# A long convolution between MLPs: the front half with taps on TensorE, the filter's transpose through DRAM, and an order written by hand

## The chip, the cores and the metric

The kernel runs on one core of a Trainium2 chip. The metric is the device time of one execution in microseconds (us), lower being better. Engine names: PE is TensorE, DVE VectorE, ACT ScalarE, POOL GpSimd, and SP SyncE, which here only issues DMAs.

## The reference

```python
def _A_ref(q, k, v, shift_k, ssm_k, ssm_D):
    ...
    for t in range(ks):
        k_shift = k_shift + k_pad[:, t:t + S, :] * shift_k[:, ks - 1 - t][None, None, :]
    kv = k_shift * v
    ...
    y_f = kv_f * kf_f[None, :, :, :]
    ...
    y = y + kv * ssm_D[None, None, :]
    return q * y

x = A_q
x = x + _A_ref(_layernorm(x, axis=-1), A_k, A_v, A_shift_k, A_ssm_k, A_ssm_D)
x = x + _B_ref(_layernorm(x, axis=-1), B_w1, B_b1, B_w2, B_b2)
x = x + _A_ref(_layernorm(x, axis=-1), A_k, A_v, A_shift_k, A_ssm_k, A_ssm_D)
x = x + _B_ref(_layernorm(x, axis=-1), B_w1, B_b1, B_w2, B_b2)
```

Sequence S = 2048, width D = 512, MLP width 1376, bf16. `kv` is a causal convolution of `k` over four taps, times `v`. It is then convolved over the whole sequence with a filter `ssm_k` of length 2048 per channel, by Fourier transforms; `_B_ref` is layernorm, a linear layer, GELU and a linear layer. The convolved `y` doesn't depend on x, so that it is worked out once for both layers.

## The kernel before

The 2048-point transform is done in two matmul stages. Stage 1 multiplies by `Ft` (the sum over 32 of the index's parts), a transpose of 32 x 32 blocks on VectorE brings the other part onto the partitions, and stage 2 multiplies by `Wt`, one 128 x 128 table for each of 32 values of k. This is done for the filter (`Kraw` -> `Ktok` -> `ZT` -> `ZK`) and for `kv` (`uv` -> `ZT` -> `ZX`). The x loop then takes the spectrum of `kv` two k at a time: `x_mul` (stage 2 into `px`, copied to `xb`, and two products with `ZK` and with `KSW`, which is `ZK` with its two halves of partitions swapped by DMA), and `x_inv` (the inverse table `Mt`, back into `ZX`). Four block transposes give `V2`, and matmuls with `Gt` give `YA` = y.

In order: all loads are issued from SP, ACT and POOL; `k_transpose` turns the filter on the PE; for each chunk `cc` of 128 channels `kv_chunk` makes the four taps on VectorE (products with a broadcast of `shift_k`, sums, product with `v`), then `stage1` is called for the filter and for `kv`. Then 16 `k_stage2`, 16 steps of the x loop with the first layernorm after the fourth, the inverse transposes, and 8 groups of the last stage. Behind that lies the MLP: `prep`, `ln_transpose`, `mm1`, `mm2` over 2 layers x 4 groups of 512 tokens. Within the program the scheduler of the language sets each engine's order; an engine works through its own queue in order, and PSUM tiles come from pools of two buffers, `pa` and `pb`.

## Time and profile before

| | us |
|---|---|
| median of 3 runs | 340.16 |
| lowest and highest | 338.97, 341.21 |
| the profiled execution | 341.24 |
| its span, first to last instruction | 339.2 |
| PE busy | 242.7 |
| VectorE busy | 225.4 |
| ScalarE busy | 164.4 |
| GpSimd busy | 19.8 |

The span is what the trace covers; the device time is 2.04 us longer. Busy times are sums over the whole span, in which stages with different limits follow one another, so a stage is read by itself. In the rows below a line number is that of the kernel before; `arena` is the one large SBUF tile in which most named buffers are placed, so that it stands for several of them. PEclk is the share of TensorE's full clock of 2.4 GHz that was granted, 0.50 being 1.2 GHz.

### The profile page before, as it was taken

Reading aid. Unit: us, or ns where it says so; the run is one execution under the profiler, and the core shown is the slowest. Engines: PE = TensorE matmul, PEld = TensorE weight load, DVE = VectorE, ACT = ScalarE, POOL = GpSimd, SP = SyncE. Lnnn points to the kernel's source line nnn. Section 1 sums busy time; section 2 is a strip of 40 time slices with the busy share of each in tenths; the row PEclk is TensorE's granted clock in tenths of the full one; section 3 lists DMA queues with packets and bytes.
Section 4 is the critical chain, followed back from the end, with each engine's and each line's share of the span. In section 5 each row is a group of like instructions: output and inputs, shape, how many; then the busy total and the mean of one; then the engine's idle time right before and its main releaser. Section 6 shows DMA issues by size and latency. Waiting matters only on the chain.

```text
span 339.2 us, 3467 instructions
## 1 busy us (share of the span) xinstructions
PE 242.7 (72%) x1292; PEld 122.0 (36%) x1312; DVE 225.4 (66%) x361; ACT 164.4 (48%) x206; POOL 19.8 (6%) x26
## 2 busy tenths in 40 slices
...
GB/s 228 372 389 4 2 0 2 0 0 247 144 255 225 122 166 166 0 0 0 2 0 0 3 0 0 2 0 1 3 0 0 2 0 46 17 41 21 18 62 46
DMA packets 7040, 21.94 MB, mean 65 GB/s; under 512 B 912, under 2 KB 4593, under 8 KB 5872
## 3 DMA queue, kind: packets, MB, share of 16 engines
...
q0 software_dynamic: 112, 0.00, 0.1%
...
## 4 chain that ended last, share of the span: by engine, by line
DVE 44%; PE 36%; DMA 8%; ACT 6%; POOL 3%; issue 2%; another core or an unknown queue 0%; DVEq 0%; POOLq 0%; ACTq 0%
PE po L328 17%; PE ph L316 14%; DVE arena L200 7%; DVE st L169 6%; DMA arena<-in_A_ssm_k_dram 6%; DVE arena L266 5%; DVE arena L177 4%; DVE kvm L159 3%; ACT arena L207 3%; DVE kvt L158 3%; DVE T L235 3%; POOL rs L173 3%; DVE arena L244 3%; DVE T L234 2%; DMA arena<-in_A_k_dram 2%
## 5 line engine op out<-in xcount | busy, mean ns | idle before, releaser
L328 PE MATMUL po<-arena 128*128 128x512 bf16 (+1 forms) x339 | 79.6, 379 | 1.9 <-DVE arena L331 1.2
L316 PE MATMUL ph<-arena 128*128 128x512 bf16 (+1 forms) x349 | 79.6, 387 | 0.8 <-ACT arena L308 0.7
L318 ACT ACTIVATE arena<-ph,B 128x512 bf16<-128x512 f32 (+1 forms) x88 | 60.3, 687 | 29.6 <-PE ph L316 27.6
L331 DVE TENSOR_TENSOR arena<-po,arena 128x512 bf16<-128x512 f32 x32 | 21.9, 683 | 50.1 <-PE po L328 50.1
L316 PEld LDWEIGHTS <-arena 128*128 128x128 bf16 (+1 forms) x352 | 35.8, 102 | 43.6 <-issue 4.2
L328 PEld LDWEIGHTS <-arena 128*128 128x128 bf16 (+1 forms) x352 | 33.8, 98 | 38.7 <-issue 1.3
L198 PE MATMUL pz<-arena,Ft 128*128 128x128 bf16 x256 | 26.1, 276 | 27.9 <-DVE arena L160 17.3
L169 DVE BATCH_NORM_STATS2 st<-arena 128x6 f32<-128x512 bf16 x64 | 42.4, 677 | 5.0 <-DMA arena<-in_A_q_dram 4.3
L199 ACT ACTIVATE ZT<-pz 128x1024 bf16<-128x1024 f32 x32 | 30.8, 1028 | 23.1 <-PE pz L198 22.7
L308 ACT ACTIVATE arena<-pt 128x512 bf16<-128x512 bf16 x32 | 17.3, 594 | 42.6 <-PE pt L307 39.5
L198 PEld LDWEIGHTS <-Ft 128*128 128x128 bf16 x256 | 22.9, 128 | 31.2 <-issue 26.9
L200 DVE STREAM_TRANSPOSE arena<-ZT 128x2048 f32<-128x2048 f32 x8 | 29.4, 3678 | 3.8 <-ACT ZT L199 3.8
L173 POOL TENSOR_TENSOR rs<-rs,mhalf 128x4 f32<-128x4 f32 x16 | 16.2, 1010 | 203.7 <-DVE rs L172 203.7
L187 PE MATMUL pk<-IDt,arena 128*128 128x128 bf16 x64 | 5.8, 265 | 27.8 <-DVE arena L143 26.7
L177 DVE TENSOR_SCALAR arena<-arena,rs,nm 128x512 bf16<-128x512 bf16 x64 | 22.1, 408 | 0.6
L273 PE MATMUL py<-arena,Gt 128*128 128x512 bf16 x31 | 9.4, 460 | 18.3 <-DVE arena L266 17.6
L242 PE MATMUL pv<-T,arena 128*128 128x512 bf16 x63 | 18.5, 392 | 3.4 <-DVE T L234 1.5
L274 ACT ACTIVATE arena<-py 128x1024 bf16<-128x1024 f32 x8 | 7.9, 1022 | 22.1 <-PE py L273 22.1
L232 ACT ACTIVATE xb<-px 128x1024 bf16<-128x1024 f32 x16 | 16.3, 1040 | 3.4 <-DVE T L235 3.3
L207 ACT ACTIVATE arena<-pk 128x1024 bf16<-128x1024 f32 x16 | 15.1, 1055 | 2.6 <-PE pk L206 2.6
L266 DVE STREAM_TRANSPOSE arena<-arena 128x2048 f32<-128x2048 f32 x4 | 16.2, 4151 | 0.1
L189 ACT ACTIVATE arena<-pk 128x2048 bf16<-128x2048 bf16 x4 | 7.2, 1882 | 18.4 <-PE pk L187 18.4
...
## 6 DMA issues: line engine op xcount, KB each, us to landing
arena<-arena SPq DMA_DIRECT2D x8, 512.0 KB, 7.7
...
arena<-in_A_ssm_k_dram ACTq DMA_DIRECT2D x4, 512.0 KB, 19.5
...
```

The costliest lines, as they stand in the source:

```text
L169: nc.vector.bn_stats(st[:, i, :], x_t[:, GT * g + i, :])
L173: nc.gpsimd.tensor_tensor(rs[:], rs[:], mhalf[:], ALU.pow)
L177: nc.vector.tensor_scalar(out=dst[:, i, :], in0=x_t[:, GT * g + i, :], scalar1=rs[:, i:i + 1], scalar2=nm[:, i:i + 1], op0=ALU.mult, op1=A ...
L198: nc.tensor.matmul(pz[:, i, :], Ft[:, q // 2, :], src[:, tau, c0:c0 + CW], start=True, stop=True)
L199: nc.scalar.activation(ZT[:, 8 * q:8 * q + 8, :], pz[:], AF.Copy)
L200: nc.vector.transpose(dst[:, :, c0:c0 + CW].bitcast(F32).rearrange("p k c -> p c k"), ZT[:].bitcast(F32).rearrange("p b c -> p c b"))
L207: nc.scalar.activation(ZK[:, 2 * j:2 * j + 2, :], pk[:], AF.Copy)
L266: nc.vector.transpose(V2[:, :, c0:c0 + CW].bitcast(F32).rearrange("p k c -> p c k"), ZX[:, :, c0:c0 + CW].bitcast(F32).rearrange("p b c -> ...
L316: nc.tensor.matmul(ph[0:m, :], W1t[:, ct, ft * P:ft * P + m], lt[:, ct, :], start=ct == 0, stop=ct == CT - 1)
L318: nc.scalar.activation(ht[0:m, ft, :], ph[0:m, :], AF.Gelu_apprx_tanh, bias=B1[0:m, ft:ft + 1])
L328: nc.tensor.matmul(po[:], ht[0:m, ft, i * P:(i + 1) * P], W2t[0:m, ft, :], start=ft == 0, stop=ft == FT - 1)
L331: nc.vector.tensor_tensor(xs, po[:], xs, ALU.add)
```

## The change

- Loads: the filter comes first on SP, then `k` in four parts, `v`, `Wt`, `Gt`; on ACT only the identity, `Ft` and the taps `sT` in 128 x 4 x 4. The broadcast `SKr`/`SK` and the shifted copy `kh` go.
- The taps: `kv_transpose` turns `k` on the PE into `kT`; GpSimd makes 16 diagonal matrices `DG`; `kv` accumulates four matmuls per tile in PSUM and VectorE multiplies the sum with `v`.
- The filter's stage 1 works on all 512 channels at a time (`k_filter_stage1`), writes its result to a buffer `Zd` in DRAM and reads it back transposed into `ZK`; the four block transposes of the filter on VectorE go.
- `kv`, stage 1 of `kv`, the block transposes and `k_stage2` are interleaved chunk by chunk. The x loop runs over two halves of 256 channels with four k per step and two steps in flight. Evictions are dealt to ScalarE (A) or VectorE (D) by the tables `E_...`.
- The statistics of the first layernorm stand behind the x loop, its scaling behind the inverse transposes.
- The order of PE, ACT and DVE in this half is that of the code (`manual_schedule`). The MLP and its order stay.

```diff
-    nc.sync.dma_start(SKr[:], apf(A_shift_k, 0, [[0, P], [1, D * KS]]))
-    nc.sync.dma_start(kh[:, KS - 1:, :], k_d.rearrange(TOK, p=P))
-    h = KS - 1
-    for p0, n in ((1, 112), (113, 15)):
-        nc.scalar.dma_start(kh[p0:p0 + n, 0:h, :], apf(k_d, (16 * p0 - h) * D, [[16 * D, n], [1, h * D]]))
-    nc.vector.memset(kh[0:1, 0:h, :], 0.0)
...
     nc.scalar.dma_start(IDt[:], ident_h.ap().bitcast(BF16))
+    nc.scalar.dma_start(Ft[:], F_h.ap().bitcast(BF16))
+    nc.scalar.dma_start(sT[:], A_shift_k.rearrange("(ct p) k -> p ct k", p=P))
     for ct in range(CT):
-        nc.scalar.dma_start(Kraw[:, ct, :], A_ssm_k[ct * P:(ct + 1) * P, :])
+        nc.sync.dma_start(Kraw[:, ct, :], A_ssm_k[ct * P:(ct + 1) * P, :])
+    for t4 in range(4):
+        nc.sync.dma_start(kn[:, 4 * t4:4 * t4 + 4, :], k_d.rearrange(TOK, p=P)[:, 4 * t4:4 * t4 + 4, :])
     nc.sync.dma_start(uv[:], v_d.rearrange(TOK, p=P))
...
-    nc.vector.tensor_copy(B1[:], b1T[:])
     nc.gpsimd.memset(mhalf[:], -0.5)
-    nc.vector.tensor_copy(SK[:], SKr[:].rearrange("p d k -> p k d"))
+    nc.vector.memset(kT[:, :, :, 0:2], 0.0)
     nc.vector.tensor_tensor(Kraw[:, :, 0], Kraw[:, :, 0], Dc[:], ALU.add)
...
-    def kv_chunk(cc):
-        c0 = cc * CW
-        m = rot.tile([P, NT, CW], BF16, name="kvm", tag="kvm")
...
-        nc.vector.tensor_tensor(m[:], kh[:, h:h + NT, c0:c0 + CW], sb(0), ALU.mult)
-        for t in range(1, KS):
-            m2 = rot.tile([P, NT, CW], BF16, name="kvt", tag="kvt")
-            nc.vector.tensor_tensor(m2[:], kh[:, h - t:h - t + NT, c0:c0 + CW], sb(t), ALU.mult)
-            nc.vector.tensor_tensor(m[:], m[:], m2[:], ALU.add)
-        nc.vector.tensor_tensor(uv[:, :, c0:c0 + CW], m[:], uv[:, :, c0:c0 + CW], ALU.mult)
...
+        def k_filter_transpose(t4):
+            pk = nxt(pa, [4, D], BF16)
...
+            evac(E_KT[t4], Ktok[:, t4 * 4:t4 * 4 + 4, :], pk[:])
+
+        def k_filter_stage1(q):
+            ZT = nxt(ZTb, [8, D])
+            for i2 in range(4):
+                pz = nxt(pb, [2, D])
+                for i in range(2):
+                    tau = 8 * (q % 2) + 2 * i2 + i
+                    nc.tensor.matmul(pz[:, i, :], Ft[:, q // 2, :], Ktok[:, tau, :], start=True, stop=True)
+                evac(E_S1K[q][i2], ZT[:, 2 * i2:2 * i2 + 2, :], pz[:])
+            for g in range(4):
+                nc.sync.dma_start(apf(Zd, (32 * g + 8 * q) * NA * D, [[D, 32], [NA * D, 8], [1, D]]),
+                                  ZT[32 * g:32 * g + 32])
...
+        def kv_transpose(t4):
+            pk = nxt(pa, [4, CT, P], BF16)
...
+            evac(E_kT[t4], kT[:, :, 4 * t4:4 * t4 + 4, 2:2 + P].rearrange("p ct i c -> p i ct c"), pk[:])
...
+        def kv(ct, o):
+            pu = nxt(pa, [8, P])
+            for i in range(8):
+                for t in range(KS):
+                    tau = 8 * o + i - t
+                    w = kT[:, ct, tau, 2:2 + P] if tau >= 0 else kT[:, ct, tau + NT, 1:1 + P]
+                    nc.tensor.matmul(pu[:, i, :], w, DG[:, ct, t, :], start=t == 0, stop=t == KS - 1)
+            us = uv[:, 8 * o:8 * o + 8, ct * P:(ct + 1) * P]
+            nc.vector.tensor_tensor(us, pu[:], us, ALU.mult)
...
+        def stage1(cc):
             c0 = cc * CW
...
+            ZT = nxt(ZTb, [NA, CW])
...
+                if q % 2 and cc < 3:
+                    kv(cc + 1, q // 2)
+                pz = nxt(pb, [8, CW])
...
+                    nc.tensor.matmul(pz[:, i, :], Ft[:, q // 2, :], uv[:, tau, c0:c0 + CW], start=True, stop=True)
+                evac(E_S1U[cc][q], ZT[:, 8 * q:8 * q + 8, :], pz[:])
+            return ZT
+
+        def z_transpose(cc, ZT):
+            c0 = cc * CW
+            nc.vector.transpose(ZX[:, :, c0:c0 + CW].bitcast(F32).rearrange("p k c -> p c k"),
                                 ZT[:].bitcast(F32).rearrange("p b c -> p c b"))
...
         def k_stage2(j):
-            pk = ps.tile([P, 2, D], F32, name="pk2", tag="pa")
+            pk = nxt(pb, [2, D])
...
-            nc.scalar.activation(ZK[:, 2 * j:2 * j + 2, :], pk[:], AF.Copy)
...
-        k_transpose()
-        for cc in range(NCH):
-            kv_chunk(cc)
-            stage1(Ktok, ZK, cc, "pa")
-            stage1(uv, ZX, cc, "pb")
-        Mt = place("Mt", [P, NA, 2, P], 96 * K)
-        nc.sync.dma_start(Mt[:], M_h.ap().bitcast(BF16))
...
-        for j in range(NA // 2):
-            k_stage2(j)
+            evac(E_K2[j % 4], ZK[:, 2 * j:2 * j + 2, :], pk[:])
...
-        x_t = place("x_t", [P, NT, D], 116 * K)
-        nc.sync.dma_start(x_t[:], q_d.rearrange(TOK, p=P))
...
+        def x_mul(j, c0, w):
+            n = 1024 // w
+            k0 = n * j
+            px = nxt(pa, [n, w])
+            for i in range(n):
+                nc.tensor.matmul(px[:, i, :], Wt[:, k0 + i, :], ZX[:, k0 + i, c0:c0 + w], start=True, stop=True)
+            xb = nxt(xbb, [n, w])
+            evac("A", xb[:], px[:])
+            T = nxt(Tb, [2, n, w])
+            nc.vector.tensor_tensor(T[:, 0], xb[:], ZK[:, k0:k0 + n, c0:c0 + w], ALU.mult)
+            nc.vector.tensor_tensor(T[:, 1], xb[:], KSW[:, k0:k0 + n, c0:c0 + w], ALU.mult)
             return T
...
-        pend = None
-        for j in range(NA // 2):
-            T = x_mul(j)
-            if pend is not None:
-                x_inv(j - 1, pend)
-            pend = T
-            if j == 3:
-                layernorm(lna0, 0)
...
+        def x_inv(j, c0, w, eng, T):
...
+                    nc.tensor.matmul(pv[:, i, :], Mt[:, k0 + i, r, :], T[:, r, i, :], start=r == 0, stop=r == 1)
+            evac(eng, ZX[:, k0:k0 + n, c0:c0 + w], pv[:])
...
+        E_KT, E_kT = "DDDD", "DDDD"
+        E_S1K = ["ADAA", "ADAA", "ADAA", "ADAA"]
+        E_S1U = ["AAAA", "AAAA", "AAAA", "AAAA"]
+        E_K2 = "AADA"
...
+        def step(j, c0, w, eng):
+            T = x_mul(j, c0, w)
+            pend.append((j, c0, w, eng, T))
+            if len(pend) > 2:
+                x_inv(*pend.pop(0))
...
+        with tc.manual_schedule(engines={ENG.PE, ENG.Activation, ENG.DVE}):
+            for t4 in range(4):
+                k_filter_transpose(t4)
+            nc.vector.tensor_copy(sF[:], sT[:])
+            for ct in range(CT):
+                for t in range(KS):
+                    nc.gpsimd.tensor_scalar(out=DG[:, ct, t, :], in0=IDt[:], scalar1=sF[:, ct, t:t + 1], scalar2=None,
+                                            op0=ALU.mult)
+            nc.vector.tensor_copy(B1[:], b1T[:])
+            for q in range(4):
+                k_filter_stage1(q)
+                kv_transpose(q)
+            for j4 in range(4):
+                nc.sync.dma_start(ZK[:, 8 * j4:8 * j4 + 8, :], apf(Zd, 8 * j4 * D, [[NA * D, P], [1, 8 * D]]))
+            kv(0, 0)
+            kv(0, 1)
+            zt = None
+            for cc in range(4):
+                if zt is not None:
+                    z_transpose(cc - 1, zt)
+                zt = stage1(cc)
+                if cc == 1:
+                    nc.scalar.dma_start(Mt[:], M_h.ap().bitcast(BF16))
+                if cc > 0:
+                    for j in range(4 * cc - 4, 4 * cc):
+                        k_stage2(j)
+            z_transpose(3, zt)
+            for j in range(12, 16):
+                k_stage2(j)
+            for j in range(8):
+                step(j, 0, 256, "AD"[j % 2])
+            nc.scalar.dma_start(x_t[:], q_d.rearrange(TOK, p=P))
+            for j in range(8):
+                step(j, 256, 256, "AAD"[j % 3])
+            drain()
+            nc.sync.dma_start(W1t[:], B_w1.rearrange("(ct p) f -> p ct f", p=P))
+            nc.sync.dma_start(W2t[:, 0:FT - 1, :], B_w2[0:(FT - 1) * P, :].rearrange("(ft p) d -> p ft d", p=P))
+            nc.sync.dma_start(W2t[0:FL, FT - 1, :], B_w2[(FT - 1) * P:F, :])
+            nc.sync.dma_start(W2t[FL:FL + 1, FT - 1, :], apf(B_b2, 0, [[D, 1], [1, D]]))
+            finish = ln_stats(0)
+            for cc in range(4):
+                inv_transpose(cc)
+            finish(lna0)
+            for t2 in range(8):
+                inv_stage2(2 * t2, 0, 512)
         DBG = None
```

`evac(eng, dst, src)` copies by ScalarE or VectorE, `nxt` deals out the buffers of `pa`, `pb` (two each in PSUM), `ZTb`, `xbb` (three each) in turn, and `ln_stats` is the first part of `layernorm`, up to the power on GpSimd; it returns the second as `finish`.

SP's queue from the start, before:

```order
L123 DMA SKr<-in_A_shift_k_dram 128x2048
L124 DMA arena<-in_A_k_dram 128x8192
L132 DMA arena<-in_A_v_dram 128x8192
L134 DMA Wt<-tabW 128x4096
L135 DMA Gt<-tabG 128x256
L215 DMA arena<-tabM 128x8192
L224 DMA arena<-in_A_q_dram 128x8192
L221 DMA arena<-arena 64x4096
```

The same place now (`ZT_100` to `ZT_102` are the three buffers `ZTb`, and a fourth round uses the first again):

```order
L133 DMA arena<-in_A_ssm_k_dram 128x2048 x4
L135 DMA arena<-in_A_k_dram 128x2048 x4
L136 DMA arena<-in_A_v_dram 128x8192
L137 DMA Wt<-tabW 128x4096
L138 DMA Gt<-tabG 128x256
L215 DMA Zd<-ZT_100 32x8x512 x4
L215 DMA Zd<-ZT_101 32x8x512 x4
L215 DMA Zd<-ZT_102 32x8x512 x4
...
L338 DMA arena<-Zd 128x4096 x4
L262 DMA arena<-arena 64x4096
L263 DMA arena<-arena 64x4096
```

The filter stands ahead of all, and sixteen stores to `Zd` and four loads from it stand between the tables and the first copies into `KSW` (L262, L263).

VectorE's queue from the last step of the first chunk's taps, before:

```order
L160 TENSOR_TENSOR arena<-kvm,arena 128x16x128
L158 TENSOR_TENSOR kvt<-arena,SK 128x2048 x2
L159 TENSOR_TENSOR kvm<-kvm,kvt 128x2048
L155 TENSOR_TENSOR kvm<-arena,SK 128x2048
L200 STREAM_TRANSPOSE arena<-ZT 128x64x32
L159 TENSOR_TENSOR kvm<-kvm,kvt 128x2048
L200 STREAM_TRANSPOSE arena<-ZT 128x64x32
L160 TENSOR_TENSOR arena<-kvm,arena 128x16x128
L158 TENSOR_TENSOR kvt<-arena,SK 128x2048
L200 STREAM_TRANSPOSE arena<-ZT 128x64x32
```

The same engine now, from the last two filter transposes' copies to the first block transpose (`pa_109`, `pa_110`, `pb_112` are PSUM buffers; L169 is the copy in `evac`, once for the filter's stage 1 and once for `kT`; L233 the product with `v`):

```order
L169 COPY arena<-pa_109 128x2048
L169 COPY arena<-pa_110 128x2048
L328 CAST sF<-sT 128x16
L333 CAST B_73<-b1T 128x11
L169 CAST ZT_100<-pb_112 128x1024
L169 COPY arena<-pa_109 128x4x4x128
L169 CAST ZT_101<-pb_112 128x1024
L169 COPY arena<-pa_110 128x4x4x128
...
L233 TENSOR_TENSOR arena<-pa_109,arena 128x8x128
...
L250 STREAM_TRANSPOSE arena<-ZT_101 128x64x32
```

The sums of products are gone; copies of `kT` and evictions of the filter's stage 1 alternate.

VectorE's queue around the first layernorm, before (it stands ahead of the x loop's products):

```order
L170 BN_AGGR mv<-st 128x2 x2
L172 TENSOR_SCALAR rs<-mv 128x4
L175 SCALAR_TENSOR_TENSOR nm<-mv,rs 128x4
L177 TENSOR_SCALAR arena<-arena,rs,nm 128x512 x4
L234 TENSOR_TENSOR T<-xb,arena 128x1024
L235 TENSOR_TENSOR T<-xb,arena 128x1024
L234 TENSOR_TENSOR T<-xb,arena 128x1024
L235 TENSOR_TENSOR T<-xb,arena 128x1024
```

And now, from the last product of the x loop:

```order
L275 TENSOR_TENSOR ZT_101<-xb_103,arena 128x1024
L169 CAST arena<-pb_112 128x4x256
L178 BN_STATS st<-arena 128x6
...
L179 BN_AGGR mv<-st 128x2
L181 TENSOR_SCALAR rs<-mv 128x4
L291 STREAM_TRANSPOSE arena<-arena 128x64x32 x4
L186 SCALAR_TENSOR_TENSOR nm<-mv,rs 128x4
L188 TENSOR_SCALAR arena<-arena,rs,nm 128x512 x4
```

The statistics have moved to the other end of the loop, and the scaling (L186, L188) behind the inverse transposes (L291).

## Rows read from the trace of the kernel before

**Rows 1.** Busy time by stage; columns as in its first row.

```profile
core 0: us, PE busy (x) PEld busy (x) DVE busy (x) ACT busy (x) POOL busy (x), PEclk, DMA share, GB/s
0.00:26.70 26.70, 0.00 (x0) 0.00 (x0) 4.60 (x8) 1.28 (x1) 2.69 (x8) 1.00 0.86 315
26.70:36.90 10.20, 6.37 (x72) 5.97 (x73) 10.20 (x10) 8.10 (x5) 0.00 (x0) 0.99 0.00 0
36.90:93.40 56.50, 28.82 (x255) 23.42 (x256) 52.57 (x29) 33.35 (x35) 0.00 (x0) 0.62 0.17 60
93.40:107.20 13.80, 9.75 (x28) 3.19 (x28) 4.54 (x14) 11.42 (x14) 1.04 (x1) 0.83 0.96 246
107.20:138.90 31.70, 25.12 (x90) 8.33 (x92) 28.59 (x40) 23.58 (x25) 0.00 (x0) 0.95 0.52 142
...
98.00:106.00 8.00, 5.31 (x18) 1.72 (x18) 4.21 (x14) 8.00 (x10) 1.04 (x1) 1.00 0.91 207
```

**Rows 2.** The chain that ended last, by time: start us, us, what.

```profile
97.02 10.19 ACT arena L207 x11
...
119.59 0.60 DVE T L235
120.19 1.07 DVE arena L244
...
138.91 16.20 DVE arena L266 x4
155.15 3.59 PE py L273 x8
```

**Rows 3.** Groups of instructions by line and shape, VectorE.

```profile
L169 DVE BATCH_NORM_STATS2 st<-arena 128x6 f32<-128x512 bf16 x64 | 42.4, 677 | 5.0 <-DMA arena<-in_A_q_dram 4.3
...
L200 DVE STREAM_TRANSPOSE arena<-ZT 128x2048 f32<-128x2048 f32 x8 | 29.4, 3678 | 3.8 <-ACT ZT L199 3.8
...
L159 DVE TENSOR_TENSOR kvm<-kvm,kvt 128x2048 bf16<-128x2048 bf16 x12 | 14.5, 1214 | 0.1
L158 DVE TENSOR_TENSOR kvt<-arena,SK 128x2048 bf16<-128x2048 bf16 x12 | 14.3, 1220 | 0.0
...
L244 DVE CAST arena<-pv 128x1024 bf16<-128x1024 f32 x8 | 9.8, 1219 | 0.9 <-PE pv L242 0.9
...
L155 DVE TENSOR_TENSOR kvm<-arena,SK 128x2048 bf16<-128x2048 bf16 x4 | 4.9, 1223 | 0.0
L160 DVE TENSOR_TENSOR arena<-kvm,arena 128x2048 bf16<-128x2048 bf16 x4 | 4.8, 1204 | 0.0
...
L142 DVE COPY SK<-SKr 128x2048 bf16<-128x2048 bf16 x1 | 1.2, 1228 | 5.5 <-DMA SKr<-in_A_shift_k_dram 5.5
```

**Rows 4.** DMA issues: KB each, median us from issue to landing.

```profile
arena<-arena SPq DMA_DIRECT2D x8, 512.0 KB, 7.7
...
arena<-in_B_w_dram SPq DMA_DIRECT2D x1, 1280.0 KB, 6.5
...
Dc<-in_A_ssm_D_dram POOLq DMA_DIRECT2D x1, 1.0 KB, 9.0
b1T<-in_B_b_dram POOLq DMA_DIRECT2D x1, 2.5 KB, 10.8
```

**Rows 5.** Timeline of the PE's matmuls, 26 to 104 us: start, length, count.

```profile
26.74 3.42 PE L187 MATMUL pk<-IDt,arena 128*128 128x128 bf16 x32 [26.74 <-DVE arena L143]
30.63 1.18 PE L187 MATMUL pk<-IDt,arena 128*128 128x128 bf16 x16 [0.47 <-ACT arena L189]
...
51.73 1.50 PE L198 MATMUL pz<-arena,Ft 128*128 128x128 bf16 x24 [1.55 <-DVE arena L160]
...
85.27 1.01 PE L198 MATMUL pz<-arena,Ft 128*128 128x128 bf16 x8 [0.26 <-ACT ZT L199]
...
94.22 1.06 PE L206 MATMUL pk<-arena,Wt 128*128 128x512 bf16 x2
...
103.59 0.59 PE L206 MATMUL pk<-arena,Wt 128*128 128x512 bf16 x2 [0.33 <-ACT arena L207]
```

More of the change, by code (lines that the diff above doesn't have):

```diff
@@ L13 @@
 AF = mybir.ActivationFunctionType
+ENG = mybir.EngineType
 NA, NB = 32, 64
@@ L174, in layernorm, with finish @@
         nm = rot.tile([P, GT], F32, name="nm", tag="nm")
-        nc.vector.scalar_tensor_tensor(nm[:], mv[:, :, 0], -1.0, rs[:], ALU.mult, ALU.mult)
-        for i in range(GT):
-            nc.vector.tensor_scalar(out=dst[:, i, :], in0=x_t[:, GT * g + i, :], scalar1=rs[:, i:i + 1],
-                                    scalar2=nm[:, i:i + 1], op0=ALU.mult, op1=ALU.add)
-    with tc.tile_pool(name="ps", bufs=2, space=bass.MemoryType.PSUM) as ps:
-        def k_transpose():
-            for t4 in range(NT // 4):
-                pk = ps.tile([P, 4, D], BF16, name="pk", tag="pa")
-                for i in range(4):
-                    for ct in range(CT):
-                        nc.tensor.transpose(pk[:, i, ct * P:(ct + 1) * P],
-                                            Kraw[:, ct, t4 * 4 + i::NT], IDt[:])
-                nc.scalar.activation(Ktok[:, t4 * 4:t4 * 4 + 4, :], pk[:], AF.Copy)
-        def stage1(src, dst, cc, tag):
+        def finish(dst):
+            nc.vector.scalar_tensor_tensor(nm[:], mv[:, :, 0], -1.0, rs[:], ALU.mult, ALU.mult)
+            for i in range(GT):
+                nc.vector.tensor_scalar(out=dst[:, i, :], in0=x_t[:, GT * g + i, :], scalar1=rs[:, i:i + 1],
+                                        scalar2=nm[:, i:i + 1], op0=ALU.mult, op1=ALU.add)
```

114 lines of the change are left out of this document (65 added, 49 removed).

## The prediction

> **What bounds the kernel now.** I read four views in this order: busy time by stage, the chain that ended last, the groups by line, and the PE's timeline. The stages [rows 1] show four different limits. Up to 26.70 us no matmul runs: the PE waits for the filter `Kraw`, whose load shares the DMA engines with the `shift_k` broadcast, `k` and `v`. From 26.70 to 93.40 us VectorE is busy 10.20 + 52.57 = 62.8 of 66.7 us: it is the bound, while the PE works 35.2 us of that and is granted only 0.62 of its clock in the longer part. From 93.40 to 107.20 us ScalarE evicts: eleven in a row take 10.19 us, 0.93 each [rows 2]. From 107.20 to 138.90 us VectorE bounds again, with two multiplications of 0.60 per step and an eviction of 1.07 every second step [rows 2]. Then four transposes of 16.20 us, and from 155.15 us [rows 2] the last convolution stage and the MLP, which the change leaves as it was. So all that can change lies in the first 155.15 us; behind it 339.2 - 155.15 = 184.05 us stay. The profiled execution takes 341.24 us, 2.04 above its span, and 1.1 above the median of 340.16; I sum against 341.24.
>
> **Load.** The broadcast of `shift_k`, and `k` ahead of the filter, go; the filter is now first on SP. In 26.70 us the DMA moved 315 GB/s [rows 1], or 8.4 MB; the filter's 2.1 MB at that rate are 6.7 us. `Dc`, which is added to it first, takes 9.0 us to landing [rows 4], and stands in POOL's queue as before: 10.2, so it is the later of the two unless start and receipt of the filter cost over 3 us. With 0.2 for the add the first transpose comes at 10.6 instead of 26.7. `k` and `v` (2.1 MB each, 6.7 us) follow by about 16 and 23, ahead of their use below. `sT` is new, 512 pieces of 8 bytes: `b1T`, also in small pieces, took 10.8 [rows 4], so it is there before VectorE asks for it at 18.
>
> **Filter transposes.** Four groups of 16; the first two came at 3.42 for 32, later ones at 1.18 [rows 5]. Their evictions move from ScalarE to VectorE: 2048 bf16 out of PSUM, which no row shows on VectorE. Bounds: 1.23, a bf16 copy of this size in SBUF (L142), and 2.3, two 1024-element casts out of PSUM (L244: 1.22 alone [rows 3], 1.07 in a row [rows 2]). I take 1.23, since source and destination are bf16 as in L142. Following the two PSUM buffers: groups end at 1.7, 3.4, 4.6, 6.0, the last copy at 7.3, so 17.9.
>
> **Four filter rounds.** Each round has 8 matmuls of 512 columns (two in 0.59 at full clock, so 0.21 each behind one another [rows 5]), evicted by A, D, A, A, then 16 transposes of `k` (1.18) and their copy on VectorE. In-order queues make a loop: transposes 1.2, copy 1.2, eviction D of the next round 1.2, the pair of matmuls that needs D's buffer 0.4, and 0.3 of hand-offs: 4.3 per round. The first D follows the last filter copy and two small casts and ends 8.9 after the first transpose, the fourth 3 x 4.3 later at 21.8, the last pair, transposes and copy at 25.0: 35.6 on the clock. GpSimd's 16 products for `DG` run beside this; they have 17 us and only the first four are needed at its end, so up to 4 us each they cost nothing.
>
> **`kv` and the forward stages.** Gone from VectorE: 12 + 12 + 4 + 4 tensor operations of 1.2, together 38.5, and four of the eight transposes of 3.68, 14.7 [rows 3]. In their place come 8 products out of PSUM (about 1.2 each, as L244) and, on the PE, 256 pairs of weight load and matmul. 24 pairs took 1.50 and 16 transposes 1.18 [rows 5], 0.062 to 0.074 each; I take 0.068, 2.2 per 32. Walked along the queues: two `kv` groups 4.4; chunk 0, four groups of 8 matmuls at 0.5 and two of `kv`, 6.4; chunks 1 and 2 the same 6.4 plus four `k_stage2`, whose evictions A, A, D, A over two buffers add 4.4, so 10.8 each; chunk 3 with eight `k_stage2` and the last transpose until the first product `T`, 12.7. That is 45.1, and the x loop's first `T` is at 80.7 instead of 108.2. VectorE's own work in it is 9.6 + 14.7 + 4.9 = 29 us, ScalarE's 28 x 0.93 = 26: a chain over three engines, with no single bound.
>
> **x loop.** First half: two steps take 4 x 0.60 + 1.07, 3.5, as before: 14.2 for eight steps. Second half: 14 evictions on ScalarE at 0.93 and a hand-off, 0.95, are 13.3, VectorE 11.8. 27.5 in all. The PE needs 12 matmuls of 256 columns per step: half of 0.21 each gives 1.3 of 1.7. `Mt`, `x_t` move to ScalarE's queue, 0.3 each of issue, beside a VectorE that bounds. The half-swapped copy `KSW`: the last 1 MB is asked for at 79.6 and lands by 88 (7.7 for issues queued behind one another [rows 4]); it is read at step 6, at 80.7 + 10.6 = 91.3. Covered by 3 us.
>
> **Statistics and the rest.** The first layernorm's statistics stood in a gap of VectorE and now stand between the loop and the inverse transposes: 4 x 0.64 of L169 (0.68 alone [rows 3]) and small ones, 3.0. Its scaling, 1.6, now lies behind the transposes, where VectorE has nothing to do until the last stage's matmuls, 3.59 us on the chain [rows 2], and their eviction are done. So the inverse transposes start at 80.7 + 27.5 + 3.0 = 111.2 and end at 127.4 instead of 155.15. Sum: 127.4 + 184.05 = 311.4 of span, **313.4 us** with the 2.04.
>
> **Rival 1, the copies out of PSUM run at one element per step** (2.3). Then the filter transposes end 3.7 later and every round takes 1.1 more: 313.4 + 3.7 + 4.4 = 321.5. For it: the only PSUM rows of VectorE run at that pace; against it: these read f32. The Trainium skill (VectorE: DVE Perf Modes, "The perf-mode tier table") lets a copy with an operand in PSUM reach two elements per cycle and no more; by that rule the copy is an estimated 1.2 and the sum stays 313.4, by the f32 rows' pace it is 321.5, and no run here shows which.
>
> **Rival 2, the filter's way through DRAM is late.** 4.2 MB go out in 1 KB pieces and come back only after all sixteen stores have landed. Stores can begin at 21.1, when the first round is evicted, and the first `k_stage2` is reached at 52.8. 1280 KB in 1 KB pieces took 6.5 us to landing [rows 4], 200 GB/s; the first 1 MB back takes 5.2 at that rate, so that 26.5 us remain for the stores: at 200 GB/s they need 21 and nothing is lost, below 158 GB/s each microsecond counts. At 100 GB/s the loads are 15.5 late, 329. Against it: that row is a load into SBUF, and stores have no rate here.
>
> **Rival 3, the queues slip past one another better than my walk**, since I let each hand-off cost in full. VectorE's work from 17.9 to 80.7 is 39 of 62.8 us; if the forward part took 35 instead of 45.1, it is 303.
>
> **Rival 4, slower: the PE stays at its lower clock level, 1.2 GHz, from the filter rounds to the end of the x loop.** Then 8 matmuls of 128 columns take 1.01, where 24 took 1.50, and two of 512 take 1.06 instead of 0.59 [rows 5]. The rounds grow by 4 x 1.2, the eight `kv` groups by 1.2 and the sixteen groups of stage 1 by 0.4 each, 16, and the x loop is bound by the PE, 192 matmuls of 0.21 = 40.3 instead of 27.5: 34 more, 347. It decides from 27.8, so when nearly all of that stretch is slow. For it: the mean of 0.62 between 36.90 and 93.40, where the PE was busy 28.82 of 56.50 us, in bursts behind VectorE. Against it: from 98 to 106 us the PE was busy 5.31 of 8.00 us and kept 1.00 [rows 1], and the new rounds keep it as busy, 2.9 of 4.3, the x loop 1.3 of 1.7.
>
> **How the numbers follow.** The forecast with its uncertainty of a few us (306 to 318) has 0.42; rival 1 (318 to 327) 0.23; rival 3 (296 to 306) 0.14; rival 2 (327 to 342) 0.12; rival 4 0.06; 0.03 for nothing gained, a mixture of these. The range reaches from 300, half of rival 3, to 333, half of rival 2, and leaves out about 0.2. A change within 1% can't be told from none. Faster by over 1% (below 336.8) is 0.91, within 1% 0.03, slower 0.06.
>
> **What will show it.** The first transpose near 10.6 us, not 26.7; the copies out of PSUM at 1.2 or 2.3; rounds of 4.3; the first `k_stage2` near 53 waiting for ScalarE's or VectorE's buffer and not for a DMA; a PE clock at 1.00 from there; the first `T` near 81; the inverse transposes near 111 to 127; 184 us behind them. I am wrong if a wait for `Zd` or `KSW` stands in the chain, if VectorE waits for GpSimd's `DG`, or if the clock is low in the x loop.

## The result and the profile after

The changed kernel takes 309.01 us (median of 12 runs, 308.68 to 309.38) against 340.15 for the kernel before (15 runs): a ratio of 0.909, 95% interval 0.907 to 0.911, and 31.1 us gained. The forecast was 313.4 in a range of 300 to 333. Executions of one kernel can fall into two groups over 1.5% apart, and each ratio goes by the faster group alone. The profiled execution takes 308.88 us with a span of 307.1, 32.1 below the span of before.

Busy time by stage in the kernel after, cut where the stages meet; the columns are those of [rows 1]:

```profile
core 0: us, PE busy (x) PEld busy (x) DVE busy (x) ACT busy (x) POOL busy (x), PEclk, DMA share, GB/s
0.00:10.60 10.60, 0.00 (x0) 0.00 (x0) 0.33 (x3) 1.28 (x1) 2.81 (x8) 1.00 0.78 248
10.60:18.10 7.50, 6.92 (x67) 6.28 (x69) 4.90 (x7) 0.84 (x1) 0.00 (x0) 1.00 1.07 431
18.10:34.00 15.90, 10.75 (x93) 6.34 (x94) 9.53 (x10) 11.12 (x12) 9.34 (x16) 1.00 0.93 290
34.00:75.10 41.10, 31.91 (x421) 25.40 (x425) 30.93 (x17) 28.25 (x30) 0.00 (x0) 1.00 0.84 259
75.10:103.40 28.30, 20.59 (x176) 17.16 (x176) 26.34 (x39) 22.66 (x24) 0.00 (x0) 1.00 0.65 198
103.40:106.80 3.40, 1.66 (x8) 1.03 (x8) 3.23 (x11) 1.02 (x1) 0.00 (x0) 0.55 0.45 146
106.80:123.00 16.20, 0.02 (x1) 0.02 (x1) 16.16 (x7) 0.00 (x0) 1.04 (x1) 0.50 0.00 0
123.00:307.10 184.10, 172.68 (x847) 81.13 (x863) 110.65 (x262) 87.05 (x129) 16.25 (x17) 0.97 0.04 12
```

The rows are the stages of the prediction: load, filter transposes, filter rounds, `kv` with the forward stages, x loop, statistics, inverse transposes, and the rest. From 34.00 to 75.10 us no engine is busy for more than 31.91 of 41.10 us, where before VectorE was busy for 52.57 of 56.50 [rows 1]; the last three rows are 203.7 us in which nothing of the gain lies. PEclk is 1.00 in every stage before 103.40.

Groups of instructions by line and shape, VectorE, of the same kernel (columns as in [rows 3]):

```profile
L250 DVE STREAM_TRANSPOSE arena<-ZT 128x2048 f32<-128x2048 f32 x4 | 17.1, 4269 | 0.3 <-ACT ZT L167 0.3
...
L274 DVE TENSOR_TENSOR ZT<-xb,arena 128x1024 bf16<-128x1024 bf16 x16 | 11.0, 685 | 2.5 <-ACT xb L167 2.5
...
L169 DVE COPY arena<-pa 128x2048 bf16<-128x2048 bf16 x8 | 9.7, 1225 | 8.9 <-PE pa L222 6.3 <-PE pa L203 2.5
...
L233 DVE TENSOR_TENSOR arena<-pa,arena 128x1024 bf16<-128x1024 f32 x8 | 9.5, 1208 | 5.0 <-PE pa L231 5.0
```

The copies whose price no row of before showed are L169 COPY: 1.225 us for 2048 bf16 elements per partition out of PSUM. The chain that ended last, in order of time, through one filter round and into `kv`:

```profile
18.21 1.14 DVE ZT L169
19.35 0.04 issue
19.39 0.59 PE pb L212 x2
19.98 0.91 PE pa L222 x16
20.91 0.89 DVE arena L169
21.80 0.25 issue
22.05 1.23 DVE ZT L169
...
33.99 3.69 PE pa L231 x63
...
38.13 1.79 PE pa L231 x32
```

A round is 22.05 - 18.21 = 3.84 us (four take 15.7, 3.93 each, up to 33.94), the 16 transposes of `k` in it 0.91, and a `kv` group of 32 weight loads with their matmuls 1.79, or 0.056 a pair.

### The profile page after: what moved, and what is told of

Same layout as the page of the kernel before. It is cut to its first block, busy times and chain, and to the rows that moved or that the text cites. A ratio compares the mean times of both kernels' runs of the same rounds, so it can differ in the third digit from the quotient of the medians.

```text
span 307.1 us, 4164 instructions
## 1 busy us (share of the span) xinstructions
PE 244.5 (80%) x1610; PEld 137.4 (45%) x1632; DVE 202.1 (66%) x347; ACT 152.2 (50%) x196; POOL 29.4 (10%) x42
## 4 chain that ended last, share of the span: by engine, by line
PE 54%; DVE 30%; ACT 5%; issue 5%; DMA 3%; POOL 2%; SPq 0%; ACTq 0%; DVEq 0%; POOLq 0%
PE ph L411 19%; PE po L423 19%; DVE st L178 5%; DVE arena L291 5%; PE pa L231 5%; DVE arena L169 5%; DMA arena<-in_A_ssm_k_dram 3%; DVE arena L188 3%; PE pb L244 2%; DVE ZT L274 2%; DVE ZT L275 2%; POOL rs L182 2%; PE pt L402 2%; PE pa L203 2%; DVE arena L392 2%
## 5 line engine op out<-in xcount | busy, mean ns | idle before, releaser
L178 DVE BATCH_NORM_STATS2 st<-arena 128x6 f32<-128x512 bf16 x64 | 42.4, 675 | 0.7
L167 ACT ACTIVATE ZT<-pb 128x1024 bf16<-128x1024 f32 x28 | 27.6, 1023 | 28.3 <-PE pb L212 17.5
L403 ACT ACTIVATE arena<-pt 128x512 bf16<-128x512 bf16 x32 | 17.5, 594 | 42.1 <-PE pt L402 38.9
L182 POOL TENSOR_TENSOR rs<-rs,mhalf 128x4 f32<-128x4 f32 x16 | 16.2, 1010 | 185.9 <-DVE rs L181 185.9
L167 ACT ACTIVATE arena<-pb 128x1024 bf16<-128x1024 f32 x22 | 22.1, 1028 | 7.5 <-PE pb L284 4.7
L299 PE MATMUL pa<-arena,Gt 128*128 128x512 bf16 x31 | 9.5, 457 | 18.5 <-DVE nm L186 17.8
L284 PE MATMUL pb<-ZT,arena 128*128 128x256 bf16 x128 | 17.3, 279 | 7.8 <-DVE arena L169 7.3
L188 DVE TENSOR_SCALAR arena<-arena,rs,nm 128x512 bf16<-128x512 bf16 x64 | 22.7, 417 | 0.6
L167 ACT ACTIVATE arena<-pa 128x1024 bf16<-128x1024 f32 x8 | 7.9, 1022 | 20.2 <-PE pa L299 20.2
L284 PEld LDWEIGHTS <-arena 128*128 128x128 bf16 x128 | 12.7, 99 | 10.9 <-issue 9.2
L167 ACT ACTIVATE xb<-pa 128x1024 bf16<-128x1024 f32 x16 | 16.0, 1029 | 3.1 <-ACT xb L167 1.4
L250 DVE STREAM_TRANSPOSE arena<-ZT 128x2048 f32<-128x2048 f32 x4 | 17.1, 4269 | 0.3 <-ACT ZT L167 0.3
L231 PE MATMUL pa<-DG,arena 128*128 128x128 bf16 x256 | 15.6, 219 | 1.3 <-DVE arena L169 1.3
L291 DVE STREAM_TRANSPOSE arena<-arena 128x2048 f32<-128x2048 f32 x4 | 16.2, 4151 | 0.0
L169 DVE COPY arena<-pa 128x2048 bf16<-128x2048 bf16 x8 | 9.7, 1225 | 8.9 <-PE pa L222 6.3
L231 PEld LDWEIGHTS <-arena 128*128 128x128 bf16 x256 | 14.6, 98 | 1.4 <-DVE arena L169 1.4
## 6 DMA issues: line engine op xcount, KB each, us to landing
arena<-tabM ACTq DMA_DIRECT2D x1, 2048.0 KB, 14.6
```

Of the source, the lines that this page charges most:

```text
L167: nc.scalar.activation(dst, src, AF.Copy)
L169: nc.vector.tensor_copy(dst, src)
L178: nc.vector.bn_stats(st[:, i, :], x_t[:, GT * g + i, :])
L182: nc.gpsimd.tensor_tensor(rs[:], rs[:], mhalf[:], ALU.pow)
L188: nc.vector.tensor_scalar(out=dst[:, i, :], in0=x_t[:, GT * g + i, :], scalar1=rs[:, i:i + 1], scalar2=nm[:, i:i + 1], op0=ALU.mult, op1=A ...
L231: nc.tensor.matmul(pu[:, i, :], w, DG[:, ct, t, :], start=t == 0, stop=t == KS - 1)
```

## The experiments

Three theories were set against one another. **A**: the time follows the chain of the prediction, so that each part is worth what it moves on that chain. **B**: the gain is the work taken off VectorE. **C**: it is the order written by hand. Every kernel computes the whole result. Where the first `T`, the inverse transposes and the end of the span are named, they are read from each run's trace; behind the inverse transposes 183.9 to 184.4 us remain in each trace, so that only what lies ahead of them differs. Of the code only a part of each change is shown; `...` marks what is left out.

**1. The load order alone, in the kernel before.**

```diff
+    for ct in range(CT):
+        nc.sync.dma_start(Kraw[:, ct, :], A_ssm_k[ct * P:(ct + 1) * P, :])
+    nc.scalar.dma_start(IDt[:], ident_h.ap().bitcast(BF16))
     nc.sync.dma_start(SKr[:], apf(A_shift_k, 0, [[0, P], [1, D * KS]]))
...
-    nc.scalar.dma_start(IDt[:], ident_h.ap().bitcast(BF16))
-    for ct in range(CT):
-        nc.scalar.dma_start(Kraw[:, ct, :], A_ssm_k[ct * P:(ct + 1) * P, :])
```

> The kernel before with one part of the change alone: the filter is loaded first on SP and the identity first on ACT, ahead of the broadcast, k and v. Theory A (the time follows the chain: a part is worth what it moves on it): the first filter transpose comes near 10.6 us, but VectorE, the bound up to 93 us, can start its taps only when the broadcast and k have landed, near 17 instead of 26.6 us, and had already done 3.7 us of taps in that wait; 6 to 7 us are won, about 333. Theory B (the whole gain is work taken off VectorE): no gain, 340.

Measured 330.09 us, 0.969 (0.967 to 0.971) of before: 10.6 us gained, not 6 to 7. The first transpose comes at 12.41 instead of 26.74 [rows 5], the inverse transposes at 127.64 instead of 138.91 [rows 2]. No work was taken off VectorE, so B falls for this part. A counted the work that VectorE does earlier, and missed a wait that goes: by 26.70 it has done 10.68 us instead of 4.60 [rows 1], and behind that it waits 0.6 instead of 3.8 us for ScalarE's `ZT`, so that its last forward transpose ends at 84.04 instead of 93.36. The other 2 of the 11.3 us lie between there and the inverse transposes; what they come from is not shown.

**2. The filter last, in the changed kernel.**

```diff
-    for ct in range(CT):
-        nc.sync.dma_start(Kraw[:, ct, :], A_ssm_k[ct * P:(ct + 1) * P, :])
     for t4 in range(4):
         nc.sync.dma_start(kn[:, 4 * t4:4 * t4 + 4, :], k_d.rearrange(TOK, p=P)[:, 4 * t4:4 * t4 + 4, :])
     nc.sync.dma_start(uv[:], v_d.rearrange(TOK, p=P))
+    for ct in range(CT):
+        nc.sync.dma_start(Kraw[:, ct, :], A_ssm_k[ct * P:(ct + 1) * P, :])
```

> The changed kernel with the filter's four loads behind k and v on SP. Theory A: the filter lands near 19 us instead of 10.4, the first transpose and all behind it come 8 to 9 us later: 317 to 318. Theory B (work taken off VectorE): the loads are hidden or made up for, 309 to 311.

Measured 319.92 us, 0.940 (0.938 to 0.941): 10.9 lost, as A has it in kind, which put it at 8 to 9. The first transpose moves from 10.68 to 21.21, the first `T` from 75.06 to 85.47: of 10.53 us of delay 10.41 arrive. The chain of this kernel begins so:

```profile
1.61 15.36 DMA sT<-in_A_shift_k_dram
16.98 0.02 issue
16.99 3.86 DMA arena<-in_A_ssm_k_dram
```

SP's queue waited 10.4 us for the 4 KB of taps (512 small pieces) before it could issue a load of the filter, which then landed at 20.85. So the order costs what the later landing costs, but part of that landing is the small load's doing and not that of `k` and `v`.

**3. The taps on VectorE again, in the changed kernel** (`kv_chunk` of before for `kv`; `kv_transpose`, `kT`, `DG` left out; the filter's copies all on ScalarE).

```diff
-            nc.tensor.matmul(pu[:, i, :], w, DG[:, ct, t, :], start=t == 0, stop=t == KS - 1)
-            nc.vector.tensor_tensor(us, pu[:], us, ALU.mult)
...
+            nc.vector.tensor_tensor(m2, kh[:, h - t:h - t + NT, c0:c0 + CW], sb(t), ALU.mult)
+            nc.vector.tensor_tensor(m, m, m2, ALU.add)
...
-                if q % 2 and cc < 3:
-                    kv(cc + 1, q // 2)
+                if q == 1 and cc < 3:
+                    kv_chunk(cc + 1)
```

> The changed kernel with the four taps back on VectorE: broadcast and shifted copy of k are loaded again, no transposes of k, no diagonal matmuls, ScalarE evicts all of the filter's stage 1. VectorE has 32 operations of 1.2 us for 8 products and 8 evictions or copies of 1.2. Theory A: part of that lies beside the filter rounds, where VectorE was idle or only a link of a loop; from 18 us VectorE's queue sums to 38.4 + 17.1 + 4.9 = 60.4 us, so the first product of the x loop comes at 79 to 80 instead of 75.1, and the time is 313 to 315. Theory B (each microsecond on VectorE counts): 38.5 - 9.5 - 9.7 = 19 more, 328.

Measured 321.33 us, 0.943 (0.941 to 0.945): 12.3 lost, between A and B. The same stretch in this kernel and in the changed one, from 18.10 to the first `T`:

```profile
18.10:87.00 68.90, 35.04 (x213) 19.78 (x214) 62.56 (x45) 42.89 (x46) 0.00 (x0) 0.78 0.75 238
```

```profile
18.10:75.00 56.90, 42.64 (x512) 31.72 (x516) 40.43 (x26) 39.27 (x42) 9.34 (x16) 1.00 0.86 268
```

VectorE has 22.1 us more to do, and idles 6.3 instead of 16.5 us: 10.2 of the 22.1 fell into idle time, and the rest is, but for rounding, the 12.0 by which the stretch is longer. This divides the stretch up; it does not show by itself what set its length. A took VectorE's list of 60.4 us for full: 62.56 were done, and 6.3 of waits came on top, the longest of them 2.8 for ScalarE's copies and 2.3 put down to a load. B counted work that falls into idle time. Two things besides VectorE's list changed: the addition to the filter waits for its load until 12.32 instead of 10.45, beside the loads that came back, and the PE's clock is 0.78 in this stretch, in which it is busy 35.04 of 68.90 us. What each of them is worth was not measured.

**4. The filter's block transposes on VectorE again, no `Zd`** (stage 1 of the filter per chunk of 128 channels).

```diff
-            for g in range(4):
-                nc.sync.dma_start(apf(Zd, (32 * g + 8 * q) * NA * D, [[D, 32], [NA * D, 8], [1, D]]),
-                                  ZT[32 * g:32 * g + 32])
...
+            return ZT
...
-                k_filter_stage1(q)
+                zk = k_filter_stage1(q)
                 kv_transpose(q)
...
-            for j4 in range(4):
-                nc.sync.dma_start(ZK[:, 8 * j4:8 * j4 + 8, :], apf(Zd, 8 * j4 * D, [[NA * D, P], [1, 8 * D]]))
+                nc.vector.transpose(ZK[:, :, q * CW:q * CW + CW].bitcast(F32).rearrange("p k c -> p c k"),
+                                    zk[:].bitcast(F32).rearrange("p b c -> p c b"))
```

> The changed kernel without the way through DRAM: the filter's stage 1 goes chunk by chunk and VectorE transposes its blocks, 4.2 us each, behind each copy of kT. Theory A: the transpose becomes a link of the round's loop (3.9 us), which grows to about 8: 4 x 4.2 = 16 to 17 more, 325. Theory B: the same 17 us on VectorE, 326. A rival to both: the rounds only wait at the end, and half of it is hidden, 317.

Measured 327.93 us, 0.963 (0.961 to 0.964): 18.9 lost. The first `kv` comes at 50.95 instead of 33.99. A round takes 9.2 instead of 3.93: a block transpose of 4.09 stands on the chain between two copies, and the PE, which waits 3.6 to 4.3 us for VectorE in each round, is granted 0.79 of its clock from 18 to 34 us and 0.70 from there to 51, so that 16 transposes of `k` take 1.72 (granted 0.50) instead of 0.91. Of the parts of the change taken back one at a time this costs the most, at this place in VectorE's order; no other place was tried. A (325) and B (326) lie too close together here to be parted.

**5. Every store to `Zd` made twice**, the first time into an unused buffer.

```diff
-            for g in range(4):
-                nc.sync.dma_start(apf(Zd, (32 * g + 8 * q) * NA * D, [[D, 32], [NA * D, 8], [1, D]]),
-                                  ZT[32 * g:32 * g + 32])
+            for Zx in (Zw, Zd):
+                for g in range(4):
+                    nc.sync.dma_start(apf(Zx, (32 * g + 8 * q) * NA * D, [[D, 32], [NA * D, 8], [1, D]]),
+                                      ZT[32 * g:32 * g + 32])
```

> The changed kernel with every store of the filter's stage 1 made twice, first into a second DRAM buffer that nobody reads, then into the real one. The stores' last landing moves from 41 to about 57 us and the first part of the filter is back near 61. Theory A: the first stage-2 matmul of the filter, at 48.2 us now, waits for it, so that the time rises by 11 to 13 us, 321; from that the slack of the way through DRAM in the changed kernel is read. Rival: ample slack, 309 to 311.

Measured 326.25 and 326.81 us, and 331.44 and 331.58 in two more executions. The ratio of 0.960 (0.954 to 0.966) goes by the first two: 17.5 lost, more than either expected. The profiled execution is that of 331.44, so that its trace shows what is waited for, and not the size of the loss. Its timeline, of SP and PE:

```profile
63.75 1.98 SPq L340 DMA_DIRECT2D arena<-Zd  x4
...
68.62 0.58 PE L260 MATMUL pb<-arena,Wt 128*128 128x512 bf16 x1 [16.12 <-DMA arena<-Zd]
```

The same two in the changed kernel:

```profile
41.21 2.07 SPq L338 DMA_DIRECT2D arena<-Zd  x4
...
48.24 0.38 PE L258 MATMUL pb<-arena,Wt 128*128 128x512 bf16 x1
```

The first load back waits for the last store, 22.5 us later; the first `k_stage2` comes 20.4 later, and in the changed kernel it waits for no DMA. So in the changed kernel the way through DRAM is hidden. An estimate of what it has to spare: here the first load back is used 4.9 us after its issue (63.75 to 68.62); by that it would be there at 46.1 in the changed kernel, about 2 us before the PE comes to it. It may be nearer 1, as the second load took 7.9 us to landing there and 6.8 here. Until the last store has landed, 4.2 MB from 21.07 to 41.21 are 208 GB/s, with the DMA engines 0.83 busy. Rival 2 of the prediction was that near.

**6. The order left to the scheduler** (`manual_schedule` replaced).

```diff
-        with tc.manual_schedule(engines={ENG.PE, ENG.Activation, ENG.DVE}):
+        if True:
```

> The changed kernel with the order of PE, ScalarE and VectorE left to the language's scheduler, and nothing else changed. Theory A: the parts carry the gain and the order a share of it: 312 to 320, the loss in places where an operation is put ahead of one that the chain needs (the statistics wait for their input ahead of the x loop). Theory C (the order written by hand is the gain): 330 or more.

Measured 323.24 us, 0.949 (0.944 to 0.954): 14.2 lost, of 31.1. C falls as the whole of the gain, as 17 us are gained without the hand-written order; but the order is worth more than A gave it, whose bound was passed by 3. The whole loss lies ahead of the first `T`, which comes at 89.27 instead of 75.06. Two waits in the trace bear on it. The cast of the taps stands on VectorE ahead of the addition to the filter and waits for `sT` until 13.14, so that the transposes that need the sum begin at 13.72 and not at 10.68. And the first layernorm's statistics stand ahead of the first `T`, for a `q` that is not there:

```profile
88.07 1.29 DVE L178 BATCH_NORM_STATS2 st<-arena 128x6 f32<-128x512 bf16 x2 [3.74 <-DMA arena<-in_A_q_dram]
```

These are 3.0 and at most 5.0 of the 14.2 us. The rest lies between them, where VectorE waits 4.50 and 5.04 us for ScalarE's `ZT` ahead of its last two block transposes; it was not traced to single instructions of the order.

**7. The x loop in steps of 512 channels, first with a queue of one step, then of two.**

```diff
-            if len(pend) > 2:
+            if len(pend) > 1:
...
-            for j in range(8):
-                step(j, 0, 256, "AD"[j % 2])
...
+            for j in range(16):
+                step(j, 0, 512, "AD"[j % 2])
...
```

> The changed kernel with the x loop's steps as before: two k of 512 channels, one step in flight, evictions alternating. Theory A: VectorE bounds either way at 3.5 us per two steps; the second half loses the lighter share of evictions (14.2 instead of 13.8 us) and the shallower pipeline about 1 us: 310 to 311. Theory B (less on VectorE is the gain): two evictions of 1.15 more on it, 311.3.

Measured 315.99 us, 0.929 (0.925 to 0.933): 7.0 lost, more than either expected. VectorE's timeline in its loop:

```profile
83.59 0.69 DVE L274 TENSOR_TENSOR ZT<-xb,arena 128x1024 bf16<-128x1024 bf16 x1 [0.54 <-ACT xb L167]
84.20 0.68 DVE L275 TENSOR_TENSOR ZT<-xb,arena 128x1024 bf16<-128x1024 bf16 x1
84.80 1.22 DVE L169 CAST arena<-pb 128x1024 bf16<-128x1024 f32 x1
85.94 0.68 DVE L274 TENSOR_TENSOR ZT<-xb,arena 128x1024 bf16<-128x1024 bf16 x1
```

Two more copies on VectorE are 2.3 us, and the waits on ScalarE's `xb` come in every second step, 5.5 us in all for 2.5 in the changed kernel: 5.3 of the 7. The second kernel keeps the width of 512 and gives back the depth of two and six copies on VectorE (`"AD"[j % 2] if j < 8 else "AAD"[j % 8 % 3]`):

> The run with 512 column steps came out 7 us over the changed kernel; it differed in the width, in the depth of the queue of steps (1 instead of 2) and in two more copies on VectorE. Here only the width is 512: the depth is 2 and VectorE has the same six copies. If depth and copies cost the 7 us (its trace: 8 copies for 6, 2.3 us, and a wait of 0.53 us on ScalarE's xb copy in every second step, 4 us): 308.5 to 310. If the width itself costs: 313 to 316.

Measured 309.39 us, 0.908 (0.907 to 0.910), as the changed kernel. The halves of 256 channels are worth nothing by themselves; the queue of two steps with the deal of copies is worth 7.

**8. The statistics spread over the second half's steps**, `q` loaded five steps earlier, the first half's copies dealt A, A, D.

```diff
-                step(j, 0, 256, "AD"[j % 2])
+                step(j, 0, 256, "AAD"[j % 3])
+                if j == 2:
+                    nc.scalar.dma_start(x_t[:], q_d.rearrange(TOK, p=P))
...
+                if j in (2, 3, 5, 6):
+                    lnp[2](2 * (j // 4) + (j % 4 == 3 or j == 6))
```

> The changed kernel with VectorE's load at the end of the x loop lightened: the first half's evictions go A, A, D instead of alternating (two of 1.15 us less on VectorE), and the layernorm's statistics are put between the second half's steps, where ScalarE bounds, with their input loaded earlier. Theory A: VectorE from the first product to the inverse transposes takes about 28 to 29 instead of 31.7 us: 305.5 to 307. Rival: ScalarE, now with 28 evictions and copies of 0.93, bounds the loop at 29 and only the statistics' 3 us move inside without gain: 308 to 309.

Measured 309.67 us, 0.911 (0.907 to 0.915): nothing gained. A had 305.5 to 307, its rival 308 to 309. What VectorE gave up, ScalarE got: the inverse transposes start at 107.23 after a wait of 2.10 us on ScalarE's last copy, where they start at 106.75 in the changed kernel. In the changed kernel's loop VectorE is busy 26.34 and ScalarE 22.66 of 28.30 us, which leaves little room to deal between them; under the 19.6 us behind it ScalarE has one copy of 1.02 us to do, and the next run tries that place.

**9. Two of the four inverse transposes between the second half's steps**, all copies of that half on ScalarE.

```diff
-                step(j, 0, 256, "AD"[j % 2])
+                step(j, 0, 256, "AAD"[j % 3])
...
-                step(j, 256, 256, "AAD"[j % 3])
+                step(j, 256, 256, "A")
+                if j in (3, 6):
+                    inv_transpose(j // 3 - 1)
...
-            for cc in range(4):
+            for cc in range(2, 4):
                 inv_transpose(cc)
```

> In the changed kernel VectorE and ScalarE are both full in the multiplication loop (103.35 - 75.06 = 28.3 us; VectorE 32 multiplies at 0.6 and 6 copies at 1.14 are 26.1 of it), and then ScalarE idles for the 19.6 us of the statistics and the four block transposes. Here the transposes of the first two column blocks, which need only the first half's results, stand between the second half's steps, and ScalarE takes all of the second half's copies and five or six of the first's eight. Theory A (the time follows the chain, now VectorE's list): first half about 12.4 us, second half 9.7 of multiplies and 8.3 of transposes = 18, statistics 3.4, two transposes 8.1, and 1 to 3 of waits: 43 to 45 in place of 47.9, so 304 to 306.5. Rival: a 4 us transpose in VectorE's list holds the multiplies that TensorE and ScalarE wait for, as every move of copies between the two engines cost as much as it gave in the run with the spread statistics: 308 to 309.5.

Measured 308.39 us, 0.906 (0.904 to 0.908): 0.6 less, too little to be told from no gain, as the two ratios' intervals overlap. A had 304 to 306.5. ScalarE's timeline has the reason:

```profile
100.97 1.02 ACT L167 ACTIVATE arena<-pb 128x1024 bf16<-128x1024 f32 x1 [3.66 <-DVE arena L291]
...
110.25 1.94 ACT L167 ACTIVATE arena<-pb 128x1024 bf16<-128x1024 f32 x2 [3.67 <-DVE arena L291]
```

The copies into `ZX` wait for the transpose that reads other columns of the same rows. So in this kernel the layout alone was changed, the two halves of `ZX` one behind the other:

```diff
-    ZX = place("ZX", [P, NA, D], 32 * K)
+    ZXh = [place(f"ZX{i}", [P, NA, D // 2], (32 + 16 * i) * K) for i in range(2)]
+    def ZX(k, c0, w):
+        return ZXh[c0 // 256][:, k, c0 % 256:c0 % 256 + w]
...
```

> The run with two early block transposes gained 0.6 us of the 3 to 5 expected: in its trace ScalarE's copies into ZX stood still for 3.66 us during each early transpose, waiting for the transpose itself, although the transpose reads columns 0 to 127 of each row of ZX and the copies write columns 256 to 511. Here alone the layout of ZX is changed: its two halves of 256 columns lie one behind the other, not row by row, so that the two no longer interleave in addresses, and the program's waits between them go. Theory A (the wait comes from the interleaved layout): both waits gone, the loop 2 to 5 us shorter, 303.5 to 306.5. Rival (the two really hold each other up, or the multiplies behind the transposes do): the copies stay late and the time 307.5 to 309.

Measured 306.13 us (305.53 to 306.52), 0.899 (0.896 to 0.902): 2.9 below the changed kernel, and the intervals of the two ratios don't meet. ScalarE's timeline beside the first early transpose, which VectorE starts at 94.80 and takes 4.17 us for:

```profile
95.22 1.08 ACT L170 ACTIVATE arena<-pb 128x1024 bf16<-128x1024 f32 x1
96.13 1.10 ACT L170 ACTIVATE xb<-pa 128x1024 bf16<-128x1024 f32 x1
97.03 1.11 ACT L170 ACTIVATE arena<-pb 128x1024 bf16<-128x1024 f32 x1
```

The copies run on. The wait was one that the program set between regions whose addresses interleave and whose elements don't meet. Behind them, at 102.11, ScalarE waits 3.05 us for the PE, which the layout does not touch. The inverse transposes end at 119.7 instead of 122.9.

**10. All buffers behind the arena 2 KB further on** (`ROW = 152 * K // 2`), for the block transposes of `kv`, which take 4.27 us where the same shape took 3.68 before [rows 3].

> The same program with the arena 2 KB larger per partition, which only moves the addresses of the buffers behind it. The block transposes of the values took 4.27 us in the changed kernel and 3.68 before for the same shapes; two of the four lie on the chain (those at 61.9 and 69.2). If the address of the source sets the duration: near 3.7 and 307.5 to 309; if it does not: 4.2 to 4.3 and 308.7 to 309.4.

Measured 309.47 us, 0.908 (0.906 to 0.910); the transposes take 4.25. A shift of 2 KB does not matter to them.

## Why the prediction held, point by point

- **Load**: 10.6 forecast, 10.68 measured, and in part by luck. The forecast took `Dc` for the later of the two, landing at 10.2, and gave the filter 6.7 us and up to 3 for start and receipt. In the trace `Dc` took 7.6 us to landing, issued at 1.25, and the filter's last part landed at 10.33, so that the addition waited for the filter:

```profile
2.13 8.20 DMA arena<-in_A_ssm_k_dram
```

```profile
10.45 0.18 DVE L145 TENSOR_TENSOR arena<-arena,Dc 128x4 bf16<-128x4 bf16 x1 [9.43 <-DMA arena<-in_A_ssm_k_dram]
```

`Dc` came 1.3 earlier than forecast, and the filter ran into the exception that the prediction had named; the two sizes happen to agree. Experiment 2 shows that a microsecond of this stage is a microsecond of the kernel.
- **Copies out of PSUM**: 1.23 taken, 1.225 measured; rival 1 (2.3) falls. The rule of the Trainium skill that the prediction cited (VectorE: DVE Perf Modes, "The perf-mode tier table") agrees with these eight copies. The last filter copy ends at 18.05 instead of 17.9.
- **Filter rounds**: 3.93 instead of 4.3. The transposes of `k` were taken at 1.18, from a row of the filter's transposes; on the chain they take 0.91, which is most of the difference. Apart from one matmul ahead of it, `kv` starts at 33.99, not 35.6. GpSimd's 16 products take 9.34 us within the window from 18.10 to 34.00, and `kv` waits for none of them.
- **`kv` and forward stages**: 41.1 instead of 45.1, the largest miss. A `kv` group is 1.79, not 2.2; all eight stand on the chain and make 3.3 us of the 4. The rest of the walk held to about half a microsecond, and the first `k_stage2` comes at 48.24 instead of 52.8, with no DMA waited for. The price of a pair was misread from its row. Rows of the PE's timeline in the changed kernel:

```profile
32.51 0.22 PE L231 MATMUL pa<-DG,arena 128*128 128x128 bf16 x1
...
37.52 0.61 PE L244 MATMUL pb<-arena,Ft 128*128 128x128 bf16 x8
37.96 1.95 PE L231 MATMUL pa<-DG,arena 128*128 128x128 bf16 x32
39.75 1.06 PE L244 MATMUL pb<-arena,Ft 128*128 128x128 bf16 x16
```

From 8 to 16 and to 32 each further matmul adds 0.056 us, and 0.16 are left over in every row, which the next row's start does not wait for (37.96 + 1.79 = 39.75). By these numbers 24 are 1.50, just what the row before showed [rows 5], at a granted clock of 1.00. So that row already ran at 0.056 a pair; divided by its count it gave 0.062, and its mean with the filter's slower transposes (0.074) the 0.068 of the sum.
- **x loop**: 28.3 instead of 27.5. The first half takes 13.7, forecast 14.2; the second 14.6, forecast 13.3 by ScalarE's list. There VectorE makes three copies and not two, and waits twice 0.69 us for `xb`. The products with `KSW` wait for nothing. **Statistics** 3.4 instead of 3.0; **inverse transposes** 16.2; the **rest** 184.1 for 184.05.
- Sum: -1.6 up to `kv`, -4.0 in it, +1.2 in the loop and the statistics: 307.1 of span for 311.4, nearly the whole of the 4.4 us between forecast and result. The chain of the stages was right, but for what the first addition waits for; the size that was off most is the price of a PE pair.
- **Rival 4** falls: PEclk is 1.00 up to 103.40. Its 347 was also summed too low: it adds 1.2 per `kv` group, where 32 pairs in experiment 5's trace take 3.55 at a granted clock of 0.50 and 1.95 at 1.00. **Rival 2** did not occur, by an estimated 2 us (experiment 5). **Rival 3** gave the time its direction but not its reason: the stage took 41.1, between 45.1 and 35, and 3.3 of these 4 us are the shorter pairs, not hand-offs that overlap.
- Taken back one at a time in the changed kernel, load order, taps and the way through DRAM cost 10.9, 12.3 and 18.9 us, together 42 of a gain of 31. The load order is worth about the same at either end (10.6 in the kernel before). So it is the other parts that cost more alone, 12.3, 18.9 and the order's 14.2, than the 20 us that are left for them together; no run takes two of them back at once, and no share of the gain can be given to each.
